# Retention attention with a channel-mix MLP: powers of lam on GpSimd, decay tables through DRAM, loads on two queues, a new order of steps

## The chip, the cores and the metric

The kernel runs on one core of one Trainium2 chip. The metric is the device time of one launch in microseconds (us); lower is better. Engines are named as in the profile: PE is the matrix engine (PEld its weight loads), DVE is VectorE, ACT is ScalarE, POOL is GpSimd, SP is SyncE, which here only issues transfers. ACT issues transfers too, on a queue of its own.

## The reference, cut to what matters

```python
# q, k, v: (4, 8, 768, 64); lam: (8,), between 0.97 and 0.99; blocks of 64
rel = pos[:, None] - pos[None, :]
Dmask = where(rel >= 0, lam ** rel, 0)            # per head, 64 x 64
lam_pow = lam ** (pos + 1); rev_pow = lam ** (63 - pos); lam_block = lam ** 64
for b in range(12):
    intra = ((qb @ kb.T) * Dmask) @ vb
    inter = (qb * lam_pow) @ kv_state
    out[b] = intra + inter
    kv_state = lam_block * kv_state + (kb * rev_pow).T @ vb
x = out as (4, 768, 512)                          # heads side by side
xk = mu_k * x + (1 - mu_k) * x_prev               # x_prev: x one position earlier
xr = mu_r * x + (1 - mu_r) * x_prev
result = sigmoid(xr @ w_r) * (relu(xk @ w_k) ** 2 @ w_v)   # 512 -> 1024 -> 512
```

All in fp32. The tables of decays (Dmask, lam_pow, rev_pow, lam_block) depend on lam alone.

## The kernel before

The sequence is cut into six tiles n of 128 positions (two blocks), and the eight heads into four pairs hp. A tile n of all four batches passes through attention pair by pair, then through the MLP. All work is written out by hand as steps in the string ORDER; a step is a letter with two digits, and every engine executes its instructions in the order in which the steps name them, so an instruction that waits holds all that stand behind it on its engine, DMA issues included.

The steps: L loads k (for n = 0 all of q, v, k) of a pair into one of two buffers IN; N loads q and v for n > 0, in two transfers (rows 0 to 63 and 64 to 127); M clears the unused halves of that buffer (POOL). A makes scores q k (PE, tile sc); a multiplies them with the decay table Dt (DVE, tile mv); q multiplies queries with the table LP (DVE); k decays keys with PW or KD (ACT); U makes the sums k v (PE, tile u); u and w update the state (ACT, DVE, with LC, lam to the 64th); B makes the attention output (PE, tile xp). e and E (ACT, with two copies on POOL) and f and F (DVE) mix with the position before; y and x split the result into a high and a low part (ACT, DVE). R and Q multiply by w_r (PE, tile rp), s is the sigmoid; K and h are the w_k product with relu and square, p splits it; V is the w_v product (PE, tile vp), o the last multiply and the store on ACT's queue. S loads a block of 64-bit weights, c and C convert it to fp32 (ACT and POOL or DVE, then three DVE instructions), D splits it. The first digits of R, Q, A and so on are the tile n, the second the pair or part.

T steps are the tables. Before, they work so: a one-hot matrix hot is loaded, DVE doubles it into rows of powers by seven multiply-adds (tile rows, each with the next square of lam in pows), and T0 to T3 copy, for two heads each, 16 partitions of rows with shifted starts into Dt (128 x 8 x 128), on SP's queue. T writes the rows of powers to a small DRAM tensor W, T4 reads it back into LP for all partitions, and POOL copies LC out of LP. PW and KD come from POOL's pow. Z with a count issues that many matmuls on zeros into the tile idle.

Before the change all loads go through SP's queue; only the stores and no loads go through ACT's. values() takes its PSUM tile xp from the pool ps_1, which has one buffer of that name; r, k and v products use the four buffers of ps_m.

Of the kernel before, what the change touches and what calls it, by code (L numbers as in the profile page):

```python
# [33 lines left out]
def tile_retention_moe(  # L34
# [64 lines left out]

    def load_qv(n, hp):  # L100
        t = IN[hp % 2]
        for i in range(2):
            rows, cols = slice(i * 64, i * 64 + 64), slice(i * 4, i * 4 + 2)
            sync.dma_start(t[rows, cols].rearrange("p c o -> p (c o)"), qv[n - 1, hp, rows])

# [9 lines left out]
    sync.dma_start(rows[0], hot)  # L120
# [207 lines left out]

    def values(n, hp):
        mv, vs = mvs.pop((n, hp)), VS[hp % 2]  # L330
        xp = ps_1.tile([128, B, 2, 64], F32, name="xp")
# [106 lines left out]
    def v_out(n, b):  # L438
# [9 lines left out]
        S=stage_part, c=conv_exponent, C=conv_bits, D=conv_split)  # L448
    for step in ORDER.split():
        if step[0] == "T":  # L450
# [19 lines left out]

ORDER = """
Sr0 L00 cr0 Cr0 k00 Sr1 T0 Z13 A00 a00 cr1 L01 U00 u00 Sr2 T T1 Cr1 Z6 B00 E00 e00 Z1 A01 L02 cr2 k01 F00 f00 R00 a01
B01 e01 U01 u01 T2 A02 Cr2 E01 Q00 k02 f01 a02 Sr3 F01 B02 R01 Sk0 U02 cr3 E02 e02 Cr3 L03 A03 F02 R02 ck0 k03 u02 T3
f02 T4 M10 U03 a03 Ck0 B03 u03 Q01 L10 N10 L11 M11 k10 e03 U10 Sk1 E03 N11 A10 Q02 q10 u10 F03 a10 w10 ck1 R03 k11 f03
B10 U11 L12 s00 q11 Ck1 Sk2 k12 e10 A11 E10 Q03 N12 a11 s01 M12 F10 ck2 s02 f10 u11 L13 Ck2 Sk3 Sv0 Sv1 Sv2 Sv3 q12
s03 K00 K01 K02 ck3 w11 h00 B11 x10 h01 k13 U12 Ck3 A12 e11 E11 K03 K04 f11 N13 L20 F11 cv0 u12 a12 A13 w12 M13 Cv0
U13 h02 h03 B12 K05 K06 L21 p00 K07 cv1 q13 h04 M20 u13 Cv1 Dv0 N20 a13 k20 w13 h05 U20 Dv1 A20 cv2 p01 E12 y10 Cv2
h06 V00 e12 k21 f12 V02 F12 cv3 Dv2 u20 h07 Cv3 w20 p02 p03 B13 M21 Dv3 y12 y11 x11 Dr0 E13 N21 q20 L22 x12 V04 F13  # L480
V06 e13 U21 u21 A21 V01 V03 L23 V05 o00 V07 k22 o01 a20 w21 f13 R10 B20 Dr1 R11 e20 o02 o03 a21 Q10 f20 M22 x13 Dk0
E20 R12 Q11 q21 R13 F20 Q12 Dk1 N22 y13 A22 a22 s10 B21 N23 U22 M23 E21 s11 L30 Q13 Dk2 q22 F21 K10 s12 h10 s13 Dk3
K11 K12 K13 h11 h12 K14 x20 K15 u22 K16 A23 w22 e21 f21 k23 U23 q23 B22 p10 h13 K17 L31 x21 h14 p11 u23 N30 a23 h15
E22 k30 M30 F22 V10 y20 h16 p12 h17 q30 e22 V12 V14 p13 V16 f22 w23 V11 B23 y21 A30 U30 E23 e23 f23 V13 o10 F23 y22
u30 L32 M31 V15 V17 a30 B30 w30 M32 x23 k31 N31 A31 o11 o12 U31 N32 q31 o13 R20 e30 Q20 a31 x22 L33 k32 R21 Q21 R22
Q22 y23 A32 E30 k33 F30 x30 u31 f30 B31 e31 w31 U32 L40 R23 N33 s20 s21 q32 Q23 u32 s22 K20 f31 s23 w32 M33 K21 a32
K22 h20 E31 A33 F31 B32 N40 a33 U33 h21 h22 p20 x31 K23 k40 K24 h23 u33 E32 K25 M40 q40 p21 h24 K26 K27 h25 h26 q33
F32 V20 h27 p22 V22 w33 p23 y31 y30 V24 e32 f32 U40 L41 u40 A40 a40 w40 x32 B33 e33 N41 f33 V21 E33 o20 V26 k41 F33
M41 y33 B40 N42 E40 U41 A41 V23 o21 V25 o22 V27 o23 R30 a41 Q30 R31 x33 Q31 R32 Q32 R33 Q33 y32 e40 q41 F40 u41 s30
q42 s31 K30 f40 s32 s33 B41 e41 K31 K32 K33 h30 w41 h31 p30 f41 L42 k42 h32 E41 F41 M42 h33 K34 p31 A42 a42 U42 N43  # L490
u42 h34 K35 x40 K36 h35 L43 k43 B42 q43 L50 k50 N50 E42 F42 M43 w42 A43 a43 x42 K37 h36 y40 U43 u43 w43 e42 h37 f42
V30 V32 B43 p32 A50 U50 y41 e43 V34 p33 x41 V31 y42 V36 V33 V35 u50 f43 y43 q50 E43 a50 o30 L51 N51 F43 o31 o32 k51
V37 o33 U51 B50 E50 q51 L52 N52 R40 Q40 A51 x43 e50 F50 f50 u51 R41 Q41 a51 B51 k52 R42 Q42 U52 R43 Q43 E51 F51 x50
L53 N53 u52 q52 A53 s40 s41 a53 s42 A52 K40 h40 q53 K41 h41 a52 s43 k53 K42 K43 h42 p40 K44 K45 K46 h43 h44 x51 p41
h45 e51 h46 f51 p42 K47 B52 h47 U53 y50 u53 p43 y51 V40 V42 e52 V41 E52 f52 V43 V44 F52 o40 y52 V46 V45 V47 B53 o41
o42 o43 x52 e53 f53 y53 R50 Q50 R51 Q51 R52 Q52 E53 F53 x53 R53 Q53 s50 s51 K50 K51 s52 h50 s53 h51 K52 h52 K53 h53
p51 p50 K54 h54 K55 h55 K56 K57 h56 h57 p53 V50 V52 V54 p52 V51 V53 o50 o51 V56 V55 V57 o52 o53
"""


# [51 lines left out]
```

## Time and profile before

| | before |
|---|---|
| runs, us | 430.81, 430.9, 437.83 (median 430.9) |
| profiled execution, us | 435.66 |
| its span, us | 433.8 |
| granted clock, mean | 0.995 |
| SP's queue (q1) | 36.56 MB, 26.8% of 16 engines |
| ACT's queue (q10) | 6.29 MB, 3.9% of 16 engines |

All kernel code is recorded under one line (L30, the helper that keeps the order), so instructions are told apart by operation and by the names of the tiles that they write and read. A row of the timeline gives the start in us, the duration in us, engine, line, operation, out<-in, partitions x elements, the count, and in brackets how long the engine stood idle before and what ended that. Matmuls are pipelined, so a busy PE is not PE at its peak, but an idle one is a hole.

### The profile page before, as it was taken

How to read it: one execution, taken by the hardware profiler on the slowest of the kernel's cores; microseconds unless marked ns; L12 is line 12 of the kernel's file. 1: busy time of each engine (PE TensorE's matmuls, PEld its weight loads, DVE VectorE, ACT ScalarE, POOL GpSimd, SP SyncE). 2: the span in 40 equal slices, each digit the busy share in tenths (PEclk: the TensorE clock that was granted, in tenths of full speed). 3: DMA queues.
4: the chain of work that ended last, by engine and by line, in shares of the span. 5: the costliest groups of instructions: out<-in, count | busy, mean ns of one | idle time of the engine just before them, and what ended most of it. 6: DMA issues, size and time to landing. Idle time of an engine off the chain costs nothing.

```text
span 433.8 us, 7285 instructions
## 1 busy us (share of the span) xinstructions
PE 419.1 (97%) x2908; PEld 325.6 (75%) x2908; DVE 263.9 (61%) x401; ACT 203.2 (47%) x354; POOL 71.5 (16%) x141
## 2 busy tenths in 40 slices
PE   6699899999999999999999999999999999999996
PEld 3455455588888888888888888878778888888885
DVE  6757799998976675655765445667455561313411
ACT  3443677895677534264544235564343460224300
POOL 4244746541110001110101001010000000000000
PEclk9989999999999999999999999999999999999999
DMA  7969994031430303531104303233430001100001
GB/s 259 315 241 283 337 381 141 20 92 56 146 99 0 97 2 122 171 96 50 51 1 121 124 1 98 68 83 104 134 100 2 0 2 48 51 0 2 0 30 68
DMA packets 13618, 43.32 MB, mean 100 GB/s; under 512 B 1936, under 2 KB 3344, under 8 KB 12048
## 3 DMA queue, kind: packets, MB, share of 16 engines
q1 hardware_dynamic: 9984, 36.56, 26.8%
q10 hardware_dynamic: 3600, 6.29, 3.9%
q8 instruction: 23, 0.38, 0.4%
q14 instruction: 11, 0.09, 0.1%
HBM read 36.03 MB, written 6.29 MB: 98 GB/s over the span
## 4 chain that ended last, share of the span: by engine, by line
PE 90%; DMA 6%; POOL 1%; DVE 1%; ACT 1%; SPq 0%; issue 0%; DVEq 0%; POOLq 0%; ACTq 0%
PE vp L30 31%; PE kp L30 29%; PE rp L30 15%; PE xp L30 5%; PE sc L30 5%; PE u L30 4%; DMA in<-qvk 3%; DMA wst<-w_k 3%; POOL wu L30 1%; ACT wu L30 1%; SPq L30 0%; PE idle L30 0%; DVE wst L30 0%; DVE wu L30 0%; DVEq L548 0%
## 5 line engine op out<-in xcount | busy, mean ns | idle before, releaser
L30 PE MATMUL vp<-hiv,k 128*128 128x512 f32 (+1 forms) x400 | 122.1, 383 | 0.0
L30 PEld LDWEIGHTS vp<-hiv,k 128*128 128x128 f32 x400 | 74.1, 188 | 15.4 <-issue 0.7
L30 PE MATMUL vp<-lov,k 128*128 128x512 f32 (+1 forms) x200 | 76.2, 381 | 0.0
L30 PE MATMUL kp<-xh,hik 128*128 128x512 f32 x160 | 62.9, 393 | 0.0
L30 PE MATMUL kp<-xl,hik 128*128 128x512 f32 x160 | 62.3, 389 | 0.0
L30 PE MATMUL kp<-xh,lok 128*128 128x512 f32 x160 | 62.3, 389 | 0.0
L30 DVE TENSOR_TENSOR kf<-kp,kf 128x512 f32<-128x512 f32 x40 | 27.4, 689 | 43.8 <-ACT kf L30 43.6
L30 ACT ACTIVATE ts<-xp,omu 128x512 f32<-128x512 f32 x48 | 32.1, 684 | 38.0 <-PE xp L30 29.4
L30 ACT ACTIVATE kf<-kp 128x512 f32<-128x512 f32 x48 | 28.6, 595 | 44.5 <-PE kp L30 40.1
L30 ACT COPY in<-st 64x256 f32<-64x256 f32 x80 | 32.4, 404 | 30.1 <-DVE st L30 17.0
L30 PEld LDWEIGHTS vp<-lov,k 128*128 128x128 f32 x200 | 37.6, 188 | 7.0
L30 DVE TENSOR_TENSOR rt<-vp,rt 128x512 f32<-128x512 f32 (+1 forms) x25 | 16.3, 667 | 42.7 <-PE vp L30 38.4
L30 DVE TENSOR_TENSOR mv<-sc,Dt 64x512 f32<-64x512 f32 (+1 forms) x48 | 32.6, 686 | 12.0 <-PE sc L30 9.9
L30 ACT CAST xh<-ts 128x512 fp32r<-128x512 f32 x40 | 24.2, 616 | 33.4 <-DVE rt L30 28.8
L30 DVE TENSOR_TENSOR mv<-in,LP 64x256 f32<-64x256 f32 x80 | 35.9, 449 | 4.2 <-DMA in<-qv 2.6
L30 DVE SCALAR_TENSOR_TENSOR ts<-xp,smalls,ts 128x512 f32<-128x512 f32 x40 | 29.5, 747 | 12.9 <-ACT ts L30 12.5
L30 POOL COPY lastw<-ts 128x4 f32<-128x4 f32 x40 | 11.3, 283 | 151.9 <-ACT ts L30 151.6
L30 DVE TENSOR_TENSOR k<-kf,k 128x1024 fp32r<-128x1024 f32 x24 | 29.9, 1258 | 10.2 <-ACT k L30 9.9
L30 DVE TENSOR_TENSOR xl<-ts,xh 128x512 fp32r<-128x512 f32 x40 | 27.1, 687 | 13.9 <-ACT xh L30 13.7
L30 PEld LDWEIGHTS kp<-xh,hik 128*128 128x128 f32 x160 | 30.0, 188 | 6.9 <-issue 0.5
L30 PEld LDWEIGHTS kp<-xh,lok 128*128 128x128 f32 x160 | 30.0, 188 | 6.3
L30 PEld LDWEIGHTS kp<-xl,hik 128*128 128x128 f32 x160 | 30.0, 188 | 6.1
(62 smaller groups left out, 585.1 us busy)
## 6 DMA issues: line engine op xcount, KB each, us to landing
in<-kk SPq DMA_DIRECT2D x20, 512.0 KB, 4.8
in<-qv SPq DMA_DIRECT2D x40, 256.0 KB, 4.7
out<-rt ACTq DMA_DIRECT2D x23, 256.0 KB, 2.1
in<-qvk SPq DMA_DIRECT2D x4, 1024.0 KB, 6.4
wst<-w_k SPq DMA_DIRECT2D x4, 1024.0 KB, 10.6
wst<-w_v SPq DMA_DIRECT2D x4, 1024.0 KB, 11.4
wst<-w_r SPq DMA_DIRECT2D x4, 512.0 KB, 7.2
Dt<-rows SPq DMA_DIRECT2D x8, 64.0 KB, 7.1
```

What stands on the lines that cost most here:

```text
L30: return lambda *args, **kw: self.tc.keep_in_program_order(op(*args, **kw))
```

## The change

The powers come from POOL's pow directly: pows0 (128 x 2) holds heads 0 and 1, pows (128 x 8) all heads; the one-hot matrix and DVE's doublings go. W grows to one row of 256 numbers for each head, zeros in front, powers behind. ACT's queue writes the zeros, then pows0 (step T), then pows of the other six heads (T3); Dt is read from W with overlapping rows in three transfers (T0 for heads 0 and 1, T1 for 2 and 3, T2 for 4 to 7), and LP too (T4), all on ACT's queue. KD becomes a step of its own (T5). N issues its first half on SP's queue and its second on ACT's. xp of (0,1) comes from ps_m. ORDER is written anew; its last 97 steps are as they were.

```diff
     def load_qv(n, hp):
         t = IN[hp % 2]
-        for i in range(2):
+        for i, queue in enumerate((sync, scalar)):
             rows, cols = slice(i * 64, i * 64 + 64), slice(i * 4, i * 4 + 2)
-            sync.dma_start(t[rows, cols]..., qv[n - 1, hp, rows])
+            queue.dma_start(t[rows, cols]..., qv[n - 1, hp, rows])
...
-    sync.dma_start(rows[0], hot)
+    pows0 = tiny.tile([128, 2], F32, name="pows0")
+    pows = tiny.tile([128, 8], F32, name="pows")
-    W = dram.tile([8, 64], F32, name="W")
+    W = dram.tile([H, 256], F32, name="W")
     vector.memset(zeros, 0.0)
-    vector.memset(rows[1][:, 0:64], 0.0)
-    gpsimd.tensor_tensor(pows[:, 3:7], lcol.broadcast_to([128, 4]), ecol, op=ALU.pow)
+    scalar.dma_start(W[:, 0:128], zeros[0:H, 0:128])
+    gpsimd.tensor_tensor(pows0, lcol0.broadcast_to([128, 2]), ecol0, op=ALU.pow)
+    gpsimd.tensor_tensor(pows, lcol.broadcast_to([128, 8]), ecol, op=ALU.pow)
     gpsimd.tensor_tensor(PW, lrow, prow.broadcast_to([128, H]), op=ALU.pow)
-    gpsimd.tensor_tensor(KD, lrow, erow.broadcast_to([128, H]), op=ALU.pow)
-    for i in range(7):
...
     def powers(step):
         if i == "":
-            sync.dma_start(W, rows[120:128, 72:136])
+            scalar.dma_start(W[0:2, 128:256].rearrange("h (x j) -> h x j", j=2), pows0)
+        elif i == "3":
+            scalar.dma_start(W[2:H, 128:256].rearrange("h (g j) -> h g j", j=8), pows[32:128])
+        elif i == "5":
+            gpsimd.tensor_tensor(KD, lrow, erow.broadcast_to([128, H]), op=ALU.pow)
         elif i == "4":
-            sync.dma_start(LP, bass.AP(..., offset=W.offset, ap=[[0, 128], [64, H], [1, 64]]))
+            scalar.dma_start(LP, bass.AP(..., offset=W.offset + 129, ap=[[0, 128], [256, H], [1, 64]]))
 ...
         else:
-            for h in (2 * int(i), 2 * int(i) + 1):
-                x = rows[h::8, 64:192]
-                sync.dma_start(Dt[:, h], bass.AP(..., ap=[x.ap[0], [1, 8], x.ap[1]]))
+            a, b = ((0, 2), (2, 4), (4, 8))[int(i)]
+            scalar.dma_start(Dt[:, a:b], bass.AP(..., offset=W.offset + a * 256 + 1, ap=[[1, 128], [256, b - a], [1, 128]]))
...
     def values(n, hp):
-        xp = ps_1.tile([128, B, 2, 64], F32, name="xp")
+        pool, tag = (ps_m, "m") if (n, hp) == (0, 1) else (ps_1, "xp")
+        xp = pool.tile([128, B, 2, 64], F32, tag=tag, name="xp")
```

The start of ORDER before:

```
Sr0 L00 cr0 Cr0 k00 Sr1 T0 Z13 A00 a00 cr1 L01 U00 u00 Sr2 T T1 Cr1 Z6 B00 E00 e00 Z1 A01 L02 cr2 k01 F00 f00 R00 a01
B01 e01 U01 u01 T2 A02 Cr2 E01 Q00 k02 f01 a02 Sr3 F01 B02 R01 Sk0 U02 cr3 E02 e02 Cr3 L03 A03 F02 R02 ck0 k03 u02 T3
f02 T4 M10 U03 a03 Ck0 B03 u03 Q01 L10 N10 L11 M11 k10 e03 U10 Sk1 E03 N11 A10 Q02 q10 u10 F03 a10 w10 ck1 R03 k11 f03
B10 U11 L12 s00 q11 Ck1 Sk2 k12 e10 A11 E10 Q03 N12 a11 s01 M12 F10 ck2 s02 f10 u11 L13 Ck2 Sk3 Sv0 Sv1 Sv2 Sv3 q12
s03 K00 K01 K02 ck3 w11 h00 B11 x10 h01 k13 U12 Ck3 A12 e11 E11 K03 K04 f11 N13 L20 F11 cv0 u12 a12 A13 w12 M13 Cv0
U13 h02 h03 B12 K05 K06 L21 p00 K07 cv1 q13 h04 M20 u13 Cv1 Dv0 N20 a13 k20 w13 h05 U20 Dv1 A20 cv2 p01 E12 y10 Cv2
h06 V00 e12 k21 f12 V02 F12 cv3 Dv2 u20 h07 Cv3 w20 p02 p03 B13 M21 Dv3 y12 y11 x11 Dr0 E13 N21 q20 L22 x12 V04 F13
V06 e13 U21 u21 A21 V01 V03 L23 V05 o00 V07 k22 o01 a20 w21 f13 R10 B20 Dr1 R11 e20 o02 o03 a21 Q10 f20 M22 x13 Dk0
...
```

and after:

```
T5 Sr0 L00 Sr1 T cr0 L01 T0 T3 Sr2 Z13 A00 k00 U00 Cr0 T1 a00 cr1 Z3 B00 L02 u00 Sr3 T2 E00 Cr1 A01 e00 cr2 k01 a01 Z5
B01 f00 F00 e01 k02 U01 E01 Z2 A02 Cr2 a02 L03 Sk0 R00 F01 cr3 u01 U02 B02 M10 f01 Cr3 N10 A03 L10 Q00 R01 Sk1 a03 T4
e02 E02 k03 ck0 u02 f02 F02 B03 k10 U03 q10 u03 M11 A10 U10 L11 Sk2 E03 N11 Ck0 Q01 e03 a10 f03 ck1 u10 F03 Ck1 k11
R02 Q02 R03 B10 w10 ck2 Sk3 s00 L12 A11 M12 s01 Sv0 q11 U11 L13 e10 u11 Sv1 E10 Ck2 F10 ck3 w11 Q03 K00 s02 K01 Sv2
N12 a11 h00 k12 f10 B11 A12 k13 U12 s03 K02 Ck3 e11 q12 E11 h01 F11 cv0 f11 N13 u12 M13 K03 a12 B12 A13 w12 Cv0 Sv3
U13 x10 p00 h02 cv1 Dv0 Cv1 x11 N20 K04 h03 K05 K06 M20 K07 p01 h04 cv2 Dv1 L20 E12 u13 Cv2 h05 A20 V00 V02 F12 h06
a13 cv3 y10 q13 L21 e12 f12 k21 w13 k20 Cv3 B13 U20 p02 N21 V04 E13 h07 Dv2 M21 L22 A21 Dv3 p03 V06 V01 Dr0 V03 a20
F13 y11 V05 q20 V07 x13 e13 k22 u20 o00 o01 w20 f13 B20 x12 Dr1 o02 o03 U21 R10 Q10 R11 Q11 a21 R12 Q12 R13 Q13 y12
y13 Dk0 Dk1 q21 s10 s11 u21 K10 E20 N22 M22 K11 h10 s12 w21 F20 K12 e20 f20 B21 M23 s13 A22 Dk2 U22 q22 Dk3 h11 a22
...
```

More of the change, by code (lines that the diff above doesn't have):

```diff
@@ L101, in load_qv @@
         t = IN[hp % 2]
[L102 removed]
+        for i, queue in enumerate((sync, scalar)):
             rows, cols = slice(i * 64, i * 64 + 64), slice(i * 4, i * 4 + 2)
[L104 removed]
+            queue.dma_start(t[rows, cols].rearrange("p c o -> p (c o)"), qv[n - 1, hp, rows])
     def clear(n, hp):
@@ L111, in clear @@
         gpsimd.memset(t[0:64, 4 if n == 1 and hp < 2 else 5:6], 0.0)
-    smalls = tiny.tile([128, 7 + H + 2 * HP], F32, name="smalls")
+    smalls = tiny.tile([128, 14 + H + 2 * HP], F32, name="smalls")
     sync.dma_start(smalls, small)
-    rows = [work.tile([128, 200], F32, tag="rt", name="rows", bufs=4) for _ in range(2)]
-    sync.dma_start(rows[0], hot)
-    lcol, ecol, lrow, erow, prow = (smalls[:, a:b] for a, b in ((0, 1), (1, 5), (5, 13), (13, 14), (14, 15)))
-    mus = smalls[:, 7 + H:].rearrange("p (w c) -> p w c", w=2)
-    pows = tiny.tile([128, 7], F32, name="pows")
+    lcol0, ecol0, lcol, ecol, lrow, erow, prow = (
+        smalls[:, a:b] for a, b in ((0, 1), (1, 3), (3, 4), (4, 12), (12, 20), (20, 21), (21, 22)))
+    mus = smalls[:, 14 + H:].rearrange("p (w c) -> p w c", w=2)
+    pows0 = tiny.tile([128, 2], F32, name="pows0")
+    pows = tiny.tile([128, 8], F32, name="pows")
     PW = tiny.tile([128, H], F32, name="PW")
     KD = tiny.tile([128, H], F32, name="KD")
-    W = dram.tile([8, 64], F32, name="W")
+    W = dram.tile([H, 256], F32, name="W")
     one = tiny.tile([128, 1], F32, name="one")
@@ L473 @@
 ORDER = """
[L474 to L478, printed above, removed]
@@ L484 @@
[L484 to L488, printed above, removed]
@@ new lines @@
+L32 M31 V17 E23 u30 w30 F23 a30 e23 f23 B30 U31 o10 x22 y23 o11 o12 o13 A31 R20 q31 N32 L33 Q20 E30 R21 x23 u31 M32
+w31 a31 Q21 R22 Q22 R23 e30 k32 q32 U32 A32 f30 F30 B31 s20 Q23 K20 u32 x30 s21 e31 N33 s22 E31 a32 F31 w32 L40 s23
+k33 K21 K22 h20 f31 B32 M33 N40 A33 U33 h21 M40 K23 E32 u33 h22 w33 K24 p20 h23 h24 p21 F32 L41 q33 K25 x32 K26 K27
+k40 h25 V20 h26 y30 h27 e32 f32 V22 A40 U40 a33 L42 y31 y32 p23 p22 B33 e33 x31 f33 y33 k41 N41 M41 V24 V21 a40 q40
+V23 E33 k42 u40 F33 w40 o20 o21 V26 A41 a41 B40 q41 x33 E40 U41 F40 V25 o22 V27 L43 k43 M42 N42 R30 o23 u41 Q30 w41
```

45 lines of the change are left out of this document (16 added, 29 removed).

## The prediction, made before the changed kernel was run

> **What bounds the kernel now.** I read the page first, then the busy time by stretches, then the order of time in the first 62 us, and last the waits of SyncE's queue and the landings of the transfers.
>
> ```profile
> span 433.8 us, 7285 instructions
> PE 419.1 (97%) x2908; PEld 325.6 (75%) x2908; DVE 263.9 (61%) x401; ACT 203.2 (47%) x354; POOL 71.5 (16%) x141
> 0.00:62.00 62.00, 51.41 (x408) 28.65 (x410) 45.15 (x75) 31.03 (x59) 30.10 (x44) 0.97 0.88 304
> 62.00:104.00 42.00, 42.00 (x290) 28.04 (x287) 41.29 (x50) 32.44 (x51) 20.27 (x18) 1.00 0.35 100
> 104.00:430.00 326.00, 325.65 (x2215) 268.93 (x2214) 176.64 (x277) 139.72 (x247) 21.17 (x79) 1.00 0.20 61
> ```
>
> In the three stretches (columns: stretch, length, busy PE, PEld, DVE, ACT, POOL, granted clock, DMA share, GB/s) PE is busy 367.65 of 368 us after 62. The change takes no matmul of the product away, so nothing after 62 can get shorter; it can only be reached earlier, or get holes that it doesn't have. From 62 to 104 DVE is full too (41.29 of 42), which matters below. So the change is decided in the first 62 us. There PE's holes, in order of time:
>
> ```profile
> 8.58 1.16 PE L30 MATMUL sc<-in 64*128 64x128 f32 x16 [1.64 <-DMA in<-qvk]
> 10.21 1.29 DVE L30 TENSOR_TENSOR mv<-sc,Dt 128x512 f32<-128x512 f32 x2 [1.46 <-DMA Dt<-rows]
> 11.69 1.09 PE L30 MATMUL xp<-mv,in 128*64 128x128 f32 x16
> 14.15 1.16 PE L30 MATMUL sc<-in 64*128 64x128 f32 x16 [1.04 <-DMA in<-qvk]
> 21.51 1.16 PE L30 MATMUL sc<-in 64*128 64x128 f32 x16 [2.80 <-DMA in<-qvk]
> 22.60 3.34 PE L30 MATMUL rp<-wr,x 128*128 128x512 f32 x4
> 24.00:26.00 2.00, 2.00 (x5) 0.47 (x5) 1.27 (x3) 0.00 (x0) 1.42 (x2) 0.50 1.02 385
> 25.87 1.38 PE L30 MATMUL xp<-mv,in 128*64 128x128 f32 x16
> 27.18 1.98 PE L30 MATMUL rp<-wr,x 128*128 128x512 f32 x4
> 42.07 1.15 PE L30 MATMUL xp<-mv,in 128*64 128x64 f32 x32 [0.23 <-DVE x L30]
> 45.47 1.09 PE L30 MATMUL u<-in 128*64 128x128 f32 x16 [2.24 <-ACT rt L30]
> 61.33 1.09 PE L30 MATMUL u<-in 128*64 128x128 f32 x16 [0.59 <-POOL ts L30]
> ```
>
> ```profile
> 9.74 0.61 PE u L30 x16
> 11.76 1.05 PE xp L30 x16
> ```
>
> Step A00 starts at 8.58, when its input is there. A00 and U00 end at 10.36 by the chain of work (start, us, what, of which these are U00 and B00); B00 waits until 11.69 for a00, which waits for the decay table Dt (1.33 lost). A01 waits for L01 (B00's end, about 12.8, to 14.15: 1.37), A02 for L02 (2.80). After that hole the granted clock is 0.50, and the four matmuls of Q00 take 3.34 instead of 1.98, B02 1.38 instead of 1.09 (1.65 lost). Then 0.23, 2.24 at U11 and 0.59 at U12. Together 10.2 us besides the start. That is the ceiling; 2% of the time, which is about what a measurement of this kernel can tell from no change, is 8.6.
>
> Why are L01 and L02 late?
>
> ```profile
> SPq L30 <- DVE wu L30: 3.8, 1, 3.8
> 2.10 6.43 DMA in<-qvk
> 7.77 0.59 SPq L30 DMA_DIRECT2D in<-qvk  x1
> 12.88 8.50 DMA in<-qvk
> 14.51 1.53 SPq L30 DMA_DIRECT2D wst<-w_r  x1
> 6.00:8.00 2.00, 0.94 (x5) 0.20 (x2) 1.90 (x6) 0.00 (x0) 1.28 (x3) 1.00 0.98 401
> 28.00:30.00 2.00, 2.00 (x23) 1.03 (x23) 1.28 (x2) 2.00 (x5) 0.75 (x4) 1.00 0.03 13
> ```
>
> SyncE stood 3.8 us before step T0, whose rows VectorE was still building, and so issued L01 only at 7.77. L02 (12.88 to 21.38) had L01, a w_r block and Dt transfers ahead or beside it. A full queue moves about 400 GB/s (401), so 1 MB costs 2.6 us; from 28 to 30 it moved 13, so the bytes do not forbid an earlier start.
>
> **The change, part by part.**
>
> *Powers.* Off VectorE go seven row updates, two squarings and a memset.
>
> ```profile
> 4.38 2.04 DVE L30 SCALAR_TENSOR_TENSOR rows<-rows,pows 128x136 f32<-128x136 f32 x5
> 2.60 1.04 POOL L30 TENSOR_TENSOR pows<-smalls 128x4 f32<-128x4 f32 x1 [1.78 <-DMA smalls<-small]
> 3.61 1.70 POOL L30 TENSOR_TENSOR PW<-smalls 128x8 f32<-128x8 f32 x1
> 5.28 1.63 POOL L30 TENSOR_TENSOR KD<-smalls 128x8 f32<-128x8 f32 x1
> ```
>
> That is about 7 x 0.41 + 0.4 = 3.2 us of DVE, all before 6.4, where it delays only the table. GpSimd's first power narrows from 4 columns to 2: between 0 and 1.04; the line through 4 and 8 columns gives 0.7, which I take: pows0 is ready at 2.6 + 0.7 = 3.3, pows 1.7 later at 5.0, PW at 6.7, before L00 lands; KD (5.28 before) slips to about 8.4, and is first read by k10, past 25.
>
> *The table.* The new chain is pows0, its write to W, the read Dt[0:2]: two transfers one behind the other, the second held on ScalarE until the first has landed. The trace has no such write beside a full SP queue. Bounds: a landing takes 1.7 at least and 5.6 at most on ScalarE's queue, and up to 9.3 for a Dt transfer.
>
> ```profile
> DMA to landing us min/median/max: 1.7/2.0/5.6
> DMA to landing us min/median/max: 3.2/7.1/9.3
> ```
>
> (The first line is that of the tile out, the second that of Dt.) Write: middle of 1.7 and 5.6, 3.7, since the SP queue is full then. Read: near Dt's minimum, 3.5. With 0.4 to issue and ScalarE's cr0 in between: 3.4 + 3.7 + 0.4 + 3.5 = 11.0 for a00's start, against 10.21. Low end 3.4 + 1.7 + 0.4 + 2.0 = 7.5 (then A00 decides, at 9.2), high end 3.4 + 5.6 + 0.4 + 9.3 = 18.7.
>
> [...]
>
> *Loads.* hot is gone (one issue, 0.45 us) and T0 no longer stands in SyncE's way. A00 starts at 8.1. L01 is issued at about 2.6 behind the second w_r block: 8.1 + 1.5 MB at 400 GB/s = 12.1. B00 runs 12.4 to 13.5 (a00 11.0 + 1.3), so A01 starts at 13.5, 0.65 earlier than before. L02 is issued at 13.5, with only a rest ahead of it and six heads of Dt beside it. The nearest row is half its size, alone: 3.3.
>
> ```profile
> in<-kk SPq DMA_DIRECT2D x1, 512.0 KB, 3.3
> ```
>
> 3.3 + 1.3 for the other half MB + 1.0 for Dt's 384 KB = 5.6 (bounds 4.6 and the old 8.5): A02 at 19.1 against 21.51, 2.4 gained. But R00 (1.91), which ran before A02, now stands behind it, so 0.5 net. Between U01 (17.9) and 19.1 lie two idle matmuls; the hole is 1.2, not 2.8, so I count the 1.65 of the low clock as saved.
>
> *Order after A02.* U02 now precedes B02 and the loads for n=1 are issued earlier: L10 and Sk1 at about 24 instead of 29.86 and 33.87.
>
> ```profile
> 43.04 1.12 ACT L30 ACTIVATE wu<-wst 128x1024 f32<-128x1024 f32 x1 [3.30 <-DMA wst<-w_k]
> 44.05 0.90 ACT L30 ACTIVATE in<-in,KD 128x256 f32<-128x256 f32 x2
> 29.86 0.33 SPq L30 DMA_DIRECT2D in<-kk  x1
> 33.87 0.43 SPq L30 DMA_DIRECT2D wst<-w_k  x1
> ```
>
> U11 lost its 2.24 because ScalarE stood in ck1 for that w_k block with k10/k11 behind it. Issued 9 us earlier, the block is there: 2.24 and the 0.23 saved. What is late next: N12, whose half on SyncE now stands behind Sk3, L12, Sv0, L13, Sv1 and Sv2. From B10's end (my count: 40.5), 4.25 MB at 400 GB/s with 2 us of issue and landing make about 53 to 54; A12 is due at 52.3. Lost there: 1.7 instead of 0.59, so minus 1.1.
>
> *T4.* The copies of LC now stand on GpSimd ahead of e02's copies, and wait for LP, now in 256-byte runs on ScalarE's queue. LP's landing before:
>
> ```profile
> DMA to landing us min/median/max: 7.8/7.8/7.8
> ```
>
>  F02, and VectorE behind it, can wait up to 3 us. Cost nothing: PE has A03, Q00, R01, B03, U03, A10, U10 and Q01, some 10 us, before R02 needs F02. Without that cover, up to 3.
>
> *q and v by two queues.* Twenty issues of some 0.5 us move from SyncE to ScalarE, 10 of its 230 idle us, each holding ScalarE until B of the tile's last user is done. xp of (0,1) takes a buffer of the idle pool, so B01 need not await f00 and F00. Both at nothing: ScalarE's next work mostly needs that B anyway.
>
> **Sum**: A02 net of R00 0.5 (the earlier start and the table's delay are in it) + clock 1.65 + U11 and B10 2.47 - N12 1.1 + 0 = 3.5. The profiled execution took 435.66 (span 433.8), so 432.2 like for like; the median of the three runs is 430.9, so the forecast is **427.4**, its own range 425 to 430.
>
> **Rivals.**
>
> *A, more: every hole but the start closes.* With the table at its low end a00 starts at 9.2, L02 leaves at 11.8, A02 starts at 17.4 (1.7 more), and N12 arrives in time (1.7): 6.9 in all, 424.0. For: DMA idles today in 26 to 30. Against: two dependent landings beside a full queue. Chance 0.17; a third of it beyond 2%.
>
> [...] Chance 0.17.
>
> *C, nothing: VectorE gives it back.* DVE is full from 62 to 104. If it gains only its removed 3.2 us where it stood idle anyway, and T4's wait takes 3 from it, PE meets late products before 104 and the gain shrinks to 0 to 1: 430.4. For: 41.29 of 42. Against: DVE idled 16.9 in the first 62. Chance 0.16.
>
> *D, over 2% slower: the waits on ScalarE's queue.*
>
> ```profile
> L30 ACT ACTIVATE ts<-xp,omu 128x512 f32<-128x512 f32 x48 | 32.1, 684 | 38.0 <-PE xp L30 29.4
> ```
>
> Sixteen later N hold ScalarE until a B of PE is done. Today it idles 38.0 / 48 = 0.79 us before such a step; if each N makes PE late by as much, that is 12.7, less the 3.5: 440.1. It decides only if a step behind N on ScalarE is needed by PE before that B. Against: PE had no hole after 62 with ScalarE at 32.44 of 42. Chance 0.05.
>
> **How the numbers follow.** Forecast 0.45, A 0.17, B 0.17, C 0.16, D 0.05. The range reaches to B's price and a little past A's, 422.5 to 435; left out are D, B's far end (a table at 18.7) and A's beyond 422.5. Faster by over 2%: 0.06, all A; slower by over 2%: 0.05, D; within: 0.89.
>
> **What would show it.** a00 at about 11 and A02 at about 19; granted clock 1.0 throughout; no wait at U11, one of 1 to 2 us at A12; PE without holes from then on. Wrong if a00 starts after 13 (B), if PE waits for DVE between 55 and 104 (C), or if ScalarE's DMA issues end PE's waits after 104 (D).

## The result: slower, by 4.5%, and the profile after

The changed kernel took 452.9, 453.81, 454.76 and 450.42 us (median 453.36), the kernel before 432.04 (four runs): a ratio of 1.0448 [1.0399, 1.0497]. The forecast was 427.4, range 422.5 to 435.0; the prediction was wrong, in sign and in size. The profiled execution took 452.9 with a span of 451.1, against 433.8 before: 17.3 us more. (The profiled executions of four experiments were slow ones: of write16 only the write's packets and landing are read, of lc_later the places of the waits, of nosplit and k00 nothing.)

The head of the page of the kernel after, and the busy time by stretches (columns: stretch, length, busy PE, PEld, DVE, ACT, POOL, granted clock, DMA share, GB/s):

```profile
span 451.1 us, 7254 instructions
PE 423.8 (94%) x2910; PEld 331.5 (73%) x2911; DVE 259.7 (58%) x391; ACT 205.2 (45%) x354; POOL 68.3 (15%) x142
0.00:62.00 62.00, 43.37 (x344) 26.59 (x346) 33.27 (x53) 23.90 (x45) 25.72 (x42) 0.86 0.71 247
62.00:104.00 42.00, 37.89 (x211) 20.62 (x210) 34.51 (x43) 28.49 (x47) 18.49 (x16) 0.92 0.46 144
104.00:446.00 342.00, 341.58 (x2351) 283.50 (x2350) 190.88 (x295) 152.76 (x265) 24.08 (x85) 1.00 0.20 63
```

PE stood idle 451.1 - 423.8 = 27.3 us, against 433.8 - 419.1 = 14.7 before: 12.6 more. It was also busy 4.7 longer, of which 2.0 are matmuls on zeros (8.8 us against 6.8 into the tile idle) and the rest the same products at a lower clock. 12.6 + 4.7 is the whole 17.3. After 104 nothing was lost (341.58 of 342), so all of it lies early. The prediction had placed it in the first 62 us; the last of the holes, at A12, falls at 69 to 73. The waits of PE (engine, tile, waited for; us in all, times, longest):

```profile
PE xp L30 <- DVE x L30: 7.5, 1, 7.5
PE u L30 <- ACT in L30: 7.3, 1, 7.3
PE sc L30 <- DMA in<-qv: 4.1, 1, 4.1
```

Three single waits make 18.9 of the 27.3. The releasers named, VectorE and ScalarE, had themselves been waiting. The chain of work (start, us, what) names what stood at the root of each:

```profile
3.35 10.72 DMA W<-pows
...
27.87 14.06 DMA LP<-W
60.92 12.41 DMA in<-qv
```

Three transfers: the write of pows0 (T), the read of LP (T4) and the loads of q and v for A12 (N12). The timeline of the kernel after shows how each reaches PE:

```profile
14.16 0.41 ACTq L30 DMA_DIRECT2D Dt<-W  x1
15.52 0.91 ACT L30 ACTIVATE in<-in,PW 128x256 f32<-128x256 f32 x2 [10.37 <-issue]
16.08 1.52 PE L30 MATMUL u<-in 128*64 128x64 f32 x16 [7.28 <-ACT in L30]
17.63 1.29 DVE L30 TENSOR_TENSOR mv<-sc,Dt 128x512 f32<-128x512 f32 x2 [10.11 <-PE u L30]
18.92 2.02 PE L30 MATMUL xp<-mv,in 128*64 128x128 f32 x16
26.01 1.16 PE L30 MATMUL sc<-in 64*128 64x128 f32 x16 [0.35 <-DMA in<-qvk]
41.98 0.41 POOL L30 COPY LC<-LP 64x4 f32<-64x4 f32 x2 [9.34 <-DMA LP<-W]
42.45 0.19 POOL L30 COPY ts<-lastw 128x4 f32<-128x4 f32 x1
42.68 1.41 DVE L30 SCALAR_TENSOR_TENSOR x<-xp,smalls,ts 128x512 f32<-128x512 f32 x2 [8.33 <-POOL ts L30]
44.23 1.98 PE L30 MATMUL xp<-mv,in 128*64 128x128 f32 x16 [7.54 <-DVE x L30]
73.46 1.97 PE L30 MATMUL sc<-in 128*64 128x128 f32 x16 [4.11 <-DMA in<-qv]
```

First, ScalarE waits in T0 for the landing of the write (until 14.16) with k00 behind it; U00 needs k00, so PE idles 7.28, and a00 comes at 17.63. Second, GpSimd waits 9.34 for LP before it copies LC; e02's copies stand behind, then F02, and B03 can't start, because its one buffer xp is still read by F02: 7.54. Third, A12 waits 4.11 for q and v. Each of these holes also drops the clock (columns as above):

```profile
11.00:21.24 10.24, 5.16 (x37) 3.49 (x39) 3.43 (x6) 2.10 (x5) 0.00 (x0) 0.50 0.28 65
41.72:48.55 6.83, 4.32 (x49) 4.35 (x51) 5.55 (x9) 1.45 (x4) 5.11 (x9) 0.50 0.03 9
72.44:79.27 6.83, 5.81 (x35) 4.47 (x36) 4.77 (x9) 1.86 (x5) 3.81 (x3) 0.50 0.51 158
```

B00 takes 2.02 instead of 1.09 at full clock. Setting such rows against their durations before, I estimate the clock's part at about 2.0, 2.1 and 2.9 us, each good to about 1 us, so the three holes cost about 9.3, 9.6 and 7.0. (The kernel before had 1.33 + 1.37 + 2.80 of holes and 1.65 of low clock, 7.15 in all, where the first of them stands.)

### The profile page after: what moved, and what is told of

It reads as the page before. It is cut to its first block, busy times and chain, and to the rows that moved or that the text cites. A ratio compares the mean times of both kernels' runs of the same rounds, so it can differ in the third digit from the quotient of the medians.

```text
span 451.1 us, 7254 instructions
## 1 busy us (share of the span) xinstructions
PE 423.8 (94%) x2910; PEld 331.5 (73%) x2911; DVE 259.7 (58%) x391; ACT 205.2 (45%) x354; POOL 68.3 (15%) x142
## 4 chain that ended last, share of the span: by engine, by line
PE 87%; DMA 9%; ACT 1%; DVE 1%; ACTq 1%; issue 0%; SPq 0%; DVEq 0%; POOL 0%; POOLq 0%
PE vp L30 29%; PE kp L30 29%; PE rp L30 14%; PE xp L30 5%; PE sc L30 5%; PE u L30 4%; DMA LP<-W 3%; DMA in<-qv 3%; DMA W<-pows 2%; DMA in<-qvk 1%; ACTq L30 1%; ACT in L30 0%; PE idle L30 0%; DVE x L30 0%; SPq L30 0%
## 5 line engine op out<-in xcount | busy, mean ns | idle before, releaser
L30 DVE TENSOR_TENSOR kf<-kp,kf 128x512 f32<-128x512 f32 x40 | 27.3, 689 | 47.0 <-ACT kf L30 46.9
L30 DVE TENSOR_TENSOR mv<-sc,Dt 64x512 f32<-64x512 f32 (+1 forms) x48 | 32.5, 685 | 15.9 <-PE u L30 10.1
L30 DVE TENSOR_TENSOR mv<-in,LP 64x256 f32<-64x256 f32 x80 | 34.6, 433 | 5.3 <-DMA in<-qv 3.7
L30 PEld LDWEIGHTS xp<-mv,in 128*64 128x64 f32 x704 | 25.7, 142 | 16.2 <-issue 13.0
L30 PE MATMUL xp<-mv,in 128*64 128x64 f32 (+1 forms) x704 | 29.2, 236 | 7.5 <-DVE x L30 7.5
```

Source lines behind the costliest of these rows:

```text
L30: return lambda *args, **kw: self.tc.keep_in_program_order(op(*args, **kw))
```

## The experiments

Each ratio is to the kernel before, run on the same chip. Where nothing else is said, an edit starts from the kernel after.

**More engines for the write.** `e1_write16` gives the write of pows0 a slowest dimension of 64 instead of 2.

```diff
-W[0:2, 128:256].rearrange("h (x j) -> h x j", j=2), pows0
+W[0:2, 128:256].rearrange("h (x j) -> x h j", j=2), pows0
```

> Step T's write of pows0 in another order of its dimensions (64 x 2 x 2 in place of 2 x 64 x 2; pows0 and its exponents are permuted to match), same 128 pieces of 8 bytes, nothing else. Theory (pieces per engine): in the changed kernel 2 engines carry 64 pieces each, and each piece waits for one 8 KB piece of SP's queue (0.31 us); with 8 pieces per engine the pieces take 2.5 us from the first at about 7.3, the write lands near 10.3 in place of 14.07, a00 starts near 14 in place of 17.6, and the run is 3 to 4 us shorter than 452.9. Rival 1 (pieces of 8 bytes into DRAM are slow in themselves, seen in the 2.4 us between the last piece at 11.7 and the landing at 14.07): landing stays at 12.5 or later, gain under 1.5. Rival 2 (the early part is covered by a later wait): landing early, but the time the same, as L10 or LP end the next hole at the same moment.

Ratio 1.0463 [1.0371, 1.0555]: no gain. The chain shows the landing 2 us earlier, not 4:

```profile
3.39 8.74 DMA W<-pows
```

In the packets of the trace, the write of the kernel after has 128 pieces of 8 bytes, the first at 7.32 and the last at 11.70, and 2 packets of 4 bytes that close it; here the pieces go from 7.37 to 10.25, and 16 such packets close it. The profile names no engine; I read one of these from each, an estimate: 2 engines with 64 pieces each there, 16 with 8 each here. So the way from the first piece to the last is only part of the 10.72: some 4 us pass before it, and about 2 after. Nor is the gain of 2 us a fixed one: on the same 16 engines the write took 9.07 in `e5_lp_early` and 10.06 in `e17_lc_back`.

**The copies of LC later.** `e2_lc_later` moves LC's copies behind ck1.

```diff
-            gpsimd.tensor_copy(LC[half], LP...)   # in T4
+ ... f03 ck1 T6 u10 F03 ...                      # T6: the same copies
```

> GpSimd's two copies of LC are taken out of step T4 and put just before u10; the transfer of LP stays where it is. Theory (LP's late landing at 41.9 reaches PE through GpSimd: LC's copies hold e02's copies, these f02 and F02, these the one xp buffer and so B03): B03 starts at about 36.7 in place of 44.2, LP still lands at about 42, the half clock of 41.7 to 48.5 is mostly gone, and the run is 6 to 9 us shorter than 452.9. Rival (LP itself is the bound: q10 on VectorE and L10 wait for the same queue): B03 early, but U10 or A10 then waits until 41 to 42 and B10 later still, gain 2 to 5 us.

Ratio 1.0414 [1.0299, 1.0529]; the gain of 6 to 9 didn't come. The timeline shows the wait in a new place, q10 on VectorE, which reads LP itself, and then F03 and R03 behind it:

```profile
44.30 1.72 DVE L30 TENSOR_TENSOR mv<-in,LP 64x256 f32<-64x256 f32 x4 [8.64 <-DMA LP<-W]
53.68 3.78 PE L30 MATMUL rp<-wr,x 128*128 128x512 f32 x4 [4.17 <-DVE x L30]
```

So LP's landing is the bound (chain of work of this kernel), whoever meets it; the new place of the copies has a cost of its own besides, which the last experiments below take away.

```profile
28.25 16.03 DMA LP<-W
```

**N12 early.** `e3_n12` moves N12 to stand right behind L12.

```diff
-Sk3 s00 L12 A11 ... Sv0 ... L13 ... Sv1 ... Sv2 N12 a11
+Sk3 s00 L12 N12 A11 ... Sv0 ... L13 ... Sv1 ... Sv2 a11
```

> Step N12 stands right behind L12 in place of behind Sv0, L13, Sv1 and Sv2. Theory (FIFO on SP's queue: N12's half there lands at 73.3 because 3.5 MB of w_v and k stand ahead): the landing comes 8 us earlier, the wait of 4.1 at A12 and the half clock of 72.4 to 79.3 (3.4 lost) go: 5 to 7.5 us shorter than 452.9. Rival (the loads moved behind it are needed as much): the hole reappears before 110 at a product that needs w_v or n=1's last pair, gain 0 to 2 us.

447.45 against 453.36: 5.9 less, as expected; ratio 1.0362 [1.0291, 1.0433]. The wait of PE for it falls from 4.1 to 0.7:

```profile
PE sc L30 <- DMA in<-qv: 0.7, 1, 0.7
```

This part of the loss is shown.

**The three together.** `e4_all` is the sum of the edits above.

> The three edits of the other runs together. If the three holes are independent: 3.5 + 7.5 + 6 = 17 us less than 452.9, 434 to 438, within 2% of the kernel before. If they cover for each other (the same load is late whichever hole is closed): no better than the best of the three by more than 3 us, 440 or more.

443.87, ratio 1.027 [1.021, 1.033]; 9.5 less than the kernel after, not the 17 of three independent holes. The waits of PE that stay are those of the write and of LP:

```profile
PE u L30 <- ACT in L30: 5.7, 1, 5.7
PE rp L30 <- DVE x L30: 4.9, 1, 4.9
```

**LP from an emptier queue.** `e5_lp_early` is `e4_all` with T4's transfer right behind T2.

```diff
-Sr3 T2 E00 ... Sk1 a03 T4 e02
+Sr3 T2 T4 E00 ... Sk1 a03 e02
```

> As e4_all (443.9), with LP's transfer issued right behind T2, about 10 us earlier, while SP's queue is empty. Theory (a piece of ScalarE's queue pays one turn of SP's queue, so 64 pieces of 256 bytes per engine cost next to nothing on an empty queue): LP lands within 5 us of its issue, by 21 in place of 41, q10 no longer holds VectorE, the wait of 4.9 that ends with a mixed x before R goes: 5 to 7 us less than e4_all, 437 to 439. Rival (L10, N10 or the conversion of w_k is due at the same moment): the hole moves to A10, U10 or K00, and the gain is 0 to 3 us.

440.44, ratio 1.0171 [1.0103, 1.0239]; 3.4 less, under the 5 to 7 expected. Yet the transfer itself, the same 1024 pieces of 256 bytes, answers clearly (view of the tile LP, issue at 16.5 instead of 27.87):

```profile
DMA to landing us min/median/max: 4.6/4.6/4.6
```

4.6 instead of 14.06. The packets of the kernel after show two parts of the 14.06. LP's first piece leaves at 33.36, 5.5 us after its issue: N10's half, which ScalarE had issued 0.6 us before it on the same queue, goes ahead (its 64 pieces of 4 KB leave from 31.36 to 34.60). Then LP's pieces are fast while SP's queue moves little (33 to 35 us; queue, packets, MB, share of 16 engines), 811 of the 1024 in 2 us:

```profile
q10 hardware_dynamic: 858, 0.31, 81.3%
q1 hardware_dynamic: 38, 0.15, 28.0%
```

The other 213 take until 41.60, beside SP's loads: from 35 to 41 us SP's queue moved 1.77 MB in 352 packets, and ScalarE's 0.04 MB in 182. The early issue takes LP out of both, so no run tells the loads of SP's queue from N10's half, which only the split put ahead of LP. The waits that stay, before U00 and before R03:

```profile
PE u L30 <- ACT in L30: 6.1, 1, 6.1
PE rp L30 <- DVE x L30: 3.1, 1, 3.1
```

**k00 ahead of the table.** `e15_k00` is `e5_lp_early` with k00 ahead of T0 and T3 on ScalarE, so that PE goes through U00.

```diff
-L01 T0 T3 Sr2 Z13 A00 k00 U00 Cr0 T1
+L01 Sr2 Z13 A00 k00 U00 T0 T3 Cr0 T1
```

> As e5_lp_early (440.4), with k00 ahead of T0 and T3 on ScalarE, so that U00 no longer waits for the write of pows0. Theory (a00 waits for the same table, so U00's wait covers nothing else): U00 starts at about 8.7 in place of 14, B00 where it was; at most the 0.7 us of U00 is won: 439.5 to 441. Rival (the hold of ScalarE is the cost): 435 or less.

Ratio 1.0216 [1.0171, 1.026], no gain: the hole in front of U00 isn't what the write costs, the late table is, as B00 stands behind it. The trace of `e9_tables`, further down, agrees: there U00 runs at 8.28, ahead of T0, and a00 still starts only at 18.22.

**SP's queue held.** `e11_hold`, from the kernel after, lets SP wait for Dt before it issues L01, so that the write meets an emptying queue.

```diff
-T cr0 L01 T0 T3
+T cr0 T0 X L01 T3      # X: sync.dma_start of 64 bytes out of Dt
```

> The changed kernel with one small transfer more: SP copies 64 bytes of Dt to DRAM ahead of L01, so that L01, the later w_r blocks and the second write of powers are issued only when the first table has landed; the 2-engine write of pows0 is left as it is. Theory (the write waits its turns behind what stands in SP's queue): with L00 and two w_r blocks alone in the queue it is empty by 7.5, the 64 pieces then pass in 0.3 us, and the write lands between 8 and 10 in place of 14.07; a00 starts at 12 to 13.5 in place of 17.6; the run gains 2 to 5 us although L01 comes later. Rival (the two transfers are slow in themselves: 64 pieces of 8 bytes on an engine, the round trip to DRAM): landing at 12 or later, a00 after 15.5, no gain.

Ratio 1.0483 [1.0433, 1.0533]. The write is issued at 3.43 and T0, which waits for it, at 10.52: 3.6 earlier than after. a00 is 3.1 earlier, at 14.53, between the theory and its rival; but L01 comes late in turn, and nothing is gained:

```profile
14.53 1.29 DVE L30 TENSOR_TENSOR mv<-sc,Dt 128x512 f32<-128x512 f32 x2 [6.87 <-DMA Dt<-W]
21.17 2.08 PE L30 MATMUL sc<-in 64*128 64x128 f32 x16 [4.21 <-DMA in<-qvk]
```

The packets of the trace: first piece at 7.39, last at 8.09, so the 64 pieces of an engine take 0.7 us where SP's queue runs empty. So the 10.72 of the kernel after splits into 4.0 until the first piece, 4.4 from the first to the last, and 2.4 from there to the landing (2.3 here, T0's issue being taken for it). The middle part isn't 64 waits for a piece of SP's: of the 128 pieces only 35 leave from 7.3 to 11.0, beside 287 of SP's; the other 93 leave in the last 0.7 us, as SP's queue runs empty (lines in the last section). The write ends when SP's queue does: SP's last piece of that stretch leaves at 11.60, the write's at 11.70. On 16 engines the middle part was 2.9 (`e1_write16`) to 5.5 us (`e17_lc_back`). The first part was 3.8 to 4.3 in all of these kernels, and its cause is open, as that of the last.

**The tables alone.** `e9_tables` is the kernel before with only the powers and tables of the change.

```diff
-Sr0 L00 cr0 Cr0 k00 Sr1 T0 ... Sr2 T T1 ... T3 f02 T4
+T5 Sr0 L00 T cr0 Cr0 k00 Sr1 T0 T3 ... Sr2 T1 ... f02 T4    # T2 stays
```

> The kernel before with the tables alone changed (powers by GpSimd, W, Dt and LP through DRAM on ScalarE's queue, in before's order of steps, k00 ahead of T0, LP where T4 stood, behind f02); loads of q, v by SP alone, xp as before. Theory (pieces of the table wait for turns of SP's queue): a00 starts at 13 to 17 in place of 10.2, LP lands 9 us or more after its issue and holds GpSimd: 438 to 448. Rival (the tables are only harmful together with the new order, whose loads L01 and w_r fill SP's queue from 2 us on; here too little stands in the queue): 429 to 434.

450.31, ratio 1.0397 [1.0327, 1.0467], more than expected: the tables alone lose almost as much as the whole change, though in part by another way. The write holds B00 here too (8.61). But T2, for half of the heads, stands behind ScalarE's other work where this order names it (issued at 27.26, at 17.64 in the kernel after), so a02 is late and, behind it on VectorE, F01, which frees xp for B02. LP, with little beside it, landed about 5 us after its issue. (Chain, then timeline:)

```profile
3.17 11.20 DMA W<-pows
27.26 7.36 DMA Dt<-W
```

```profile
18.97 2.56 PE L30 MATMUL xp<-mv,in 128*64 128x128 f32 x16 [8.61 <-DVE mv L30]
36.81 1.97 PE L30 MATMUL xp<-mv,in 128*64 128x128 f32 x16 [6.59 <-DVE x L30]
```

**The rest of the change with the old tables.** `e6_old_tables` has the new order, the split of q and v and the change of xp, but before's tables on SP's queue, LP behind the last Dt, LC ahead of u10; `e7_old_tables_n12` also has N12 early.

```diff
+Sr0 L00 Sr1 T0 cr0 L01 T Sr2 ... T1 ... T2 T3 T4 E00 ... ck1 T6 u10     # e6
+... L12 N12 A11 ...                                                   # e7, beside it
```

> The changed kernel's order of steps, its halves of q and v on two queues and its xp buffer, but the tables made as before (one-hot rows doubled by VectorE, Dt copied from them, W and LP, all on SP's queue; LP behind the last Dt, LC's copies before u10). N12 stays late. Theory (the tables through DRAM on ScalarE's queue are the larger part of the loss; the order by itself costs only N12's hole): no hole of 7 us at U00 or at B03, 4 to 7 us lost at A12, some won before: 431 to 438. Rival (the order is itself the loss, as it needs loads in a sequence that the queue can't deliver): 444 or more, with holes at the same products as in the changed kernel.

> As e6_old_tables (442.7), with N12 right behind L12. Theory (with the tables off ScalarE's queue and N12 early, the new order has no loss left): the wait of PE for q and v at A12 and its half clock go, 5 to 7 us less than e6, 436 to 438, and so still not faster than the kernel before, as the waits for L02 and L03 stay. Rival (the split loads and the order are still late at other places): 440 or more, or, if the order does what it was built for, under 430.

442.74, ratio 1.0203 [1.0121, 1.0284], above what was expected, and 437.87, ratio 1.0119 [1.0085, 1.0152], as expected. Even without the new tables these lose. Part of that is the experiments' own (`e18_lc_back_old`); the rows of PE in the timeline of `e7_old_tables_n12` that led there, and POOL's and DVE's ahead of it:

```profile
39.92 2.77 POOL L30 TENSOR_SCALAR wu<-wu 128x1024 f32<-128x1024 f32 x1
42.64 0.43 POOL L30 COPY LC<-LP 64x4 f32<-64x4 f32 x2
43.10 0.48 DVE L30 SCALAR_TENSOR_TENSOR st<-st,LC,u 128x256 f32<-128x256 f32 x1 [1.48 <-POOL LC L30]
44.30 3.67 PE L30 MATMUL rp<-wr,x 128*128 128x512 f32 x4 [2.53 <-DVE x L30]
```

The copies of LC, ready to go since LP landed, stand behind GpSimd's 2.77 us for a w_k block; u10, F03 and R03 stand behind them.

**The split alone.** `e8_nsplit` is the kernel before with only q and v by two queues.

```diff
-        for i in range(2):
+        for i, queue in enumerate((sync, scalar)):
```

> The kernel before with one edit: the second half of each q and v load is issued by ScalarE. Theory: nothing, 430 to 434, as ScalarE's next work needs the same products. Rival (ScalarE held by the wait before each of the 20 issues makes PE late, 0.5 us or more each): 440 or more, with waits of PE for ScalarE after 62.

447.75, ratio 1.0339 [1.0268, 1.041]: the rival's size by a cause that neither had named. The timeline:

```profile
90.65 0.47 SPq L30 DMA_DIRECT2D in<-qv  x1
100.60 0.47 ACTq L30 DMA_DIRECT2D in<-qv  x1
103.81 1.97 PE L30 MATMUL u<-in 128*64 128x128 f32 x16 [7.07 <-DMA in<-qv]
132.61 1.97 PE L30 MATMUL sc<-in 128*64 128x128 f32 x16 [2.83 <-DMA in<-qv]
```

SP issues its half of N21 at 90.65. ScalarE issues the other 9.95 us later, because its program gets there only then: SyncE, which only issues, is that far ahead, and ScalarE has its other work first. No wait of PE in this run is put down to ScalarE, so the split didn't hold PE up through ScalarE's compute, as rival D had it; ScalarE held the split up.

**The same, issued earlier.** `e16_n_early` moves N21 and N22 of `e8_nsplit` ahead.

```diff
-B13 M21 Dv3 y12 y11 x11 Dr0 E13 N21      +B13 N21 M21 Dv3 y12 y11 x11 Dr0 E13
-B20 Dr1 ... Q12 Dk1 N22                  +B20 N22 Dr1 ... Q12 Dk1
```

> As e8_nsplit (447.75), with N21 named right behind B13 and N22 right behind B20. Theory (the half on ScalarE's queue is issued only when ScalarE's program comes to it; the wait for B is not the cost): ScalarE issues N21 within 2 us of SyncE, PE's wait of 7.1 at U21 and the half clock after it go, and some of the hole near 128: 6 to 12 us less, 436 to 441. Rival (ScalarE is held at N until B is done, and what stands behind it is late): no gain, 446 or more, the holes are ended by ScalarE's compute.

439.31, ratio 1.0153 [1.0115, 1.0191], 8.4 less, as expected. ScalarE's issue of N21 moves to 93.75 and the wait of 7.07 shrinks. Of the 1.5% that stay, a wait of 3.96 for q and v at 39.14 is a part; the rest wasn't traced:

```profile
93.75 0.47 ACTq L30 DMA_DIRECT2D in<-qv  x1
99.10 1.09 PE L30 MATMUL u<-in 128*64 128x128 f32 x16 [0.20 <-DMA in<-qv]
```

**The new order without the split.** `e14_nosplit` is `e7_old_tables_n12` with both halves on SP's queue.

> As e7_old_tables_n12 (437.9), with both halves of q and v on SP's queue. Theory (the new order names N at places where ScalarE comes to it as early as SyncE, so the split neither costs nor gains): 436 to 440. Rival (the split is a loss in any order, as in e8): 434 or less; and if the split was a gain there: 441 or more.

435.89, ratio 1.0065 [1.0035, 1.0094], beside 1.0119 [1.0085, 1.0152] with the split: 2 us, at the edge of what four and ten runs resolve.

**LC's copies back.** Three kernels put the copies ahead of e02, where they stand in the change, with LP read early: `e17_lc_back` on `e5_lp_early`, `e18_lc_back_old` on `e7_old_tables_n12`, `e19_lc_back_nosplit` on `e14_nosplit`.

```diff
-e02 E02 k03 ... f03 ck1 T6 u10 F03
+T6 e02 E02 k03 ... f03 ck1 u10 F03
```

> The kernel with N12 early and LP read early (e5_lp_early) took 440.44 and kept a wait of 3.08 us of PE before R03. Its timeline puts the copies of LC, which that kernel had moved behind ck1, behind GpSimd's 2.77-us step of the w_k block, and u10, F03 and R03 behind them. Here the copies go back ahead of e02, where LP has landed by then. Theory (the wait was made by the moved copies): 440.44 - 3.1 = 437.3, between 436 and 438.5, no wait of R03. Rival (F03 is late for other reasons of the new order, its place taken by the next wait): 439.5 or more.

> The same edit on the kernel with the new order, the split of q and v and the old tables (e7_old_tables_n12, 437.87), where the wait of R03 was 2.53 and its four products at half clock took 3.67 instead of 1.98. Theory (the moved copies made both): 437.87 - 2.5 - 1.7 = 433.7, between 432.5 and 435.0. Rival (the loss is in the order itself): 436.5 or more.

> The same edit on the kernel with the new order, the old tables and all of q and v on SP's queue (e14_nosplit, 435.89). Theory: 435.89 - 4.2 = 431.7, between 430.5 and 433.5, level with the kernel before or up to 0.5% better. Rival (the order itself is behind): 435 or more.

437.47, ratio 1.0117 [1.0073, 1.0161], 3.0 less, as expected, though a wait of 1.6 stays at R03; 435.04 (12 runs), ratio 1.0043 [1.0012, 1.0073], 2.8 less, at the edge of the 432.5 to 435.0 expected, with the wait down to 0.3; 434.53 (12 runs), ratio 1.0041 [1.0006, 1.0076], 1.4 less, between the theory and its rival. So the moved copies cost 1.4 to 3 us in the kernels that had them. With them back the split makes no difference (435.04 and 434.53), and the new order with the old tables is 0.4% behind the kernel before, just told from it. Its waits of PE are mostly those of the start again (`e18_lc_back_old`):

```profile
PE sc L30 <- DMA in<-qvk: 7.1, 4, 3.0
```

**What each part cost.** The medians in one row, the kernel before at 433.3 beside the last three: changed 453.36; N12 early 447.45 (5.9); then LP read early, with the write on 16 engines, which alone gained nothing, 437.47 (10.0); then the old tables 435.04 (2.4); the kernel before 433.3 (1.7, the order and the split). Runs on different chips stand side by side here, so each step is good to about 1 us. Nor is each step one cause alone: the 10.0 holds LP's way past N10's half, and up to about 1 us of the write's (T0 comes at 13.55 in `e17_lc_back`, at 14.55 in `e3_n12`), and the 2.4 is all of the new tables, their write on 16 engines, against the old ones.

**What the prediction counted as gain, alone.** `e12_sk1` takes only this from the new order: U02 ahead of R01, and the w_k block Sk1 ahead of L11.

```diff
-F01 B02 R01 Sk0 U02 cr3      +F01 B02 U02 R01 Sk0 cr3
-L10 N10 L11 M11 k10 e03 U10 Sk1 E03      +L10 N10 Sk1 L11 M11 k10 e03 U10 E03
```

> The kernel before with two steps moved, nothing of the change: U02 ahead of R01, so that L10 is issued when U02 and B02 are done, and Sk1 ahead of L11. Theory (U11's wait of 2.24 comes from ScalarE standing in ck1 until that w_k block lands at 43.0): the block is issued at about 28.5 in place of 33.87, ck1 starts by 39, U11 loses nothing, the run is 1.5 to 3 us shorter than before. Rival (the 0.5 MB of L11, now behind 1 MB of w_k, ends the same wait): 0.

432.32 (12 runs) against 433.6 (23 runs), ratio 0.9978 [0.9947, 1.0009]. The trace has no wait at U11 any more, but the gain is about 1 us, less than the 1.5 to 3 expected, and isn't told from none. `e13_sr1` adds the second block of w_r behind L01, so that L01 lands earlier.

```diff
-k00 Sr1 T0 Z13 A00 a00 cr1 L01 U00      +k00 T0 Z13 A00 a00 L01 Sr1 U00
```

> As e12_sk1, and the second w_r block is issued behind L01 (its conversion moved behind e00): 0.5 MB less stands ahead of the first Dt transfer and of L01. Theory: a00 starts at about 9.3 in place of 10.2, L01 lands 1.3 earlier (12.8), L02 is issued 1 us earlier: 1 to 2.5 us less than e12. Rival (SyncE still waits for VectorE's rows until 6.45, and the block only moves ahead of L02 in place of L01): 0, or a loss of 1 if cr1 then waits on ScalarE ahead of k01.

Ratio 1.0002 [0.9979, 1.0025]: nothing. No version tried beats the kernel before beyond the uncertainty.

## Why the prediction was wrong, step by step

**What held.** Nothing was lost after 104, and U11's wait of 2.24 did go. The powers on GpSimd cost what was said, A00 started at 7.64 (8.1 predicted), and a00 came 3.47 after T0's issue, where the read was put at 3.5. What failed were a cover, two sizes and the clock.

**T4, the largest part (10.0): "Cost nothing" had the wrong cover.** The prediction followed F02 to R02 and counted 10 us of PE's work ahead of it. But B03, which it listed as cover, also needs what F02 frees, the one buffer of xp. And LP took 14.06 instead of the 7.8 before: 5.5 until its first piece, with N10's half ahead of it on ScalarE's queue, then 213 late pieces beside SP's loads. The term allowed 3, the wait was 7.54 and half clock came behind it.

**N12 (5.9): right mechanism, size off.** It does queue behind Sv0, L13, Sv1 and Sv2. The term was 1.1; the hole is 4.11 and the half clock behind it about 2.9. The prediction's sum has 4.25 MB, but what it lists as ahead of N12, Sk3 included, makes 5.25 MB with N12's half; at its own 400 GB/s the missing 1 MB is 2.5 us, and 1.7 + 2.5 is about the hole that came. That this fits so well is partly luck: Sk3 was issued at 48.56, well before B10's end, and from 60 to 74 us the queues moved 4.48 MB at 320 GB/s, not 400.

**The write of pows0 (2.4): a term mis-sized.** The step took the middle of two landings, 3.7, with 5.6 as its upper end; it took 10.72, and a00 came at 17.63 where about 11 was predicted, A02 at 26.01 where about 19 was. The price of B, the slower kernel to which the range reaches up, was my estimate, and no run shows it: in its place the packets show pieces that go one for one with SP's until SP's queue runs empty, which is 4.4 of the 10.72, and the 2.4 comes from a kernel with the write on 16 engines and other loads. That the hole of 7.28 in front of U00 costs so little has a plain reason: most of it replaces holes that the kernel before had for L01 and L02. The two engines are my reading of 2 closing packets, against 16 in `e1_write16`. The upper end of the sum came from tile out's landings of 256 KB, which says nothing of pieces of 8 bytes beside a full queue.

**The split "at nothing": right here, for no reason of the prediction's.** In the changed order, with the old tables on SP's queue, it costs nothing that can be told (`e18_lc_back_old`, `e19_lc_back_nosplit`); with the new tables it put N10's half ahead of LP, and no run shows that kernel without it. In the order before it costs some 14 us (`e8_nsplit`), not because the 20 issues hold ScalarE, as rival D had it, but because they come when its program lets them.

**The clock: saved became lost.** The step counted 1.65 as saved. Mean granted clock went from 0.995 to 0.974. The sum had no term for what a new hole does to the clock after it.

**The gains counted, 0.5 for A02 and 2.47 for U11 and B10, did not show in the time either.** The order with the old tables, N12 early and LC's copies in place is 1.7 us behind, and U11's part taken alone (`e12_sk1`) is worth about 1.

**What stays open.** No run takes away the write's 4.0 us ahead of the first piece, nor is the time behind the last explained (2.4 in the kernel after). How much of T4's part is the split's, by N10's half, wasn't tested, and neither was the change of xp by itself. Why the new order, so mended, stays 0.4% behind the kernel before wasn't tested.

## What to carry to other kernels

Before a small transfer is put on a second queue beside a full one, count its pieces per engine and price each at one piece of the other queue, until that queue is empty (here 0.31 us beside pieces of 8 KB, 0.16 beside 4 KB); its bytes say little (1 KB took 10.72 us), and in this kernel 6 us came on top that no count of pieces explains. Where a wait is called covered, follow the chain through buffers as well as data: a product that waits for a free buffer is no cover (B03 waited 7.54). A load issued by a computing engine leaves when that engine's program reaches it (9.95 us after SP's half in `e8_nsplit`), so move it in the order when it changes its queue.

## What the runs showed of the hardware

- **One piece for one.** Beside SP's full queue, the pieces of the write went one for one with SP's pieces of 4 and 8 KB. In the kernel after, from 7.3 to 11.0 us and from 11.0 to 11.8 (queue, packets, MB, share of 16 engines):

```profile
q1 hardware_dynamic: 287, 1.57, 101.5%
q10 hardware_dynamic: 35, 0.00, 0.5%
q1 hardware_dynamic: 50, 0.14, 43.4%
q10 hardware_dynamic: 95, 0.00, 6.7%
```

  35 pieces of 8 bytes on two engines are 17.5 an engine, one each 0.21 us; 287 of SP's on 16 are 17.9. In the packets the write's pieces come in two series, 0.31 us from one to the next between 7.6 and 10.1 and 0.16 between 10.1 and 11.2; SP's pieces of 8 KB took 0.31 each and those of 4 KB 0.16. The other 93 pieces left between 11.0 and 11.7, most of them after 11.4, as SP's queue ran empty.
- **Bytes did not set the time.** The write of 1 KB took 10.72 us beside a full SP queue, the read of 256 KB 4.6 beside a nearly empty one. In the kernel after and seven of the experiments' kernels, 3.8 to 4.3 us passed from the write's issue to its first piece, and 0.6 to 2.6 from its last piece to T0's issue.
- **Half clock after short holes, but not after each.** The split's 2.83-us hole brought it for 3.4 us (`e8_nsplit`, columns as above):

```profile
132.10:135.50 3.40, 2.89 (x38) 2.92 (x40) 0.86 (x2) 0.00 (x0) 0.00 (x0) 0.50 0.00 0
```

  So did the one of 2.80 in the kernel before, for 3.41 us (23.09 to 26.50). Yet a hole of 2.69 (`e8_nsplit`, at 37.76) and one of 3.08 (`e5_lp_early`, at 48.42) brought none: the product behind the second took its 1.98 at full clock. The stretches of half clock in the kernel after lasted 10.24, 6.83 and 6.83 us. What decides whether a hole of this length costs clock, no run shows.
